# One core of attention, a gated product and an ELU layer: w_out converted first, two PSUM banks for its product, a planner that parks nothing at the shared port, and 150 priorities from a table

## The chip, the cores and the metric

The kernel runs on one core of a Trainium2 chip. Its metric is the device time of one execution in microseconds (us); the profile gives the span, from the first to the last instruction, and the time of the same execution beside it. TensorE is called PE here, VectorE DVE, ScalarE ACT, GpSimd POOL, and SyncE, which issues all DMAs of this kernel, SP.

## What is computed

Three layers in a row: block-causal attention (4 batches, 8 heads, 576 positions of 64 values), then `((x w1) * (x w2)) w3 w_out`, then an ELU layer of 2048 hidden values. All inputs are fp32.

```python
B, H, S, D = q.shape                                  # 4, 8, 576, 64
scores = scale * np.matmul(q, k.transpose(0, 1, 3, 2))
mask = block_i >= block_j                             # blocks of 64 positions
attn = softmax(np.where(mask, scores, -1000000000.0)) # in words: exp(s - max) / (sum + 1e-09)
attn_out = np.matmul(attn, v)
x = attn_out.transpose(0, 2, 1, 3).reshape(B * S, H * D)      # 2304 x 512
h = ((x @ w1) * (x @ w2)) @ w3
x = h @ w_out                                         # w1, w2: 512x1024, w3: 1024x1024, w_out: 1024x512
h = x @ w_in                                          # 512x2048
g = np.where(h > 0.0, h, np.exp(np.minimum(h, 0.0)) - 1.0)
out = g @ w_out2                                      # 2048x512
```

## The kernel before, in words

Every fp32 product runs as three faster matmuls on a rounded high part and a remainder (`PASSES`). So each operand is split: activations on the way (a cast, then a subtraction), weights by `convert`, in units of 128x512. A unit is loaded by SP as 64-bit words into one of four places (tile `cr`), ACT does one or two passes over it (L315, L322), DVE three (L328, L331, L336, with the middle result `cp` in a PSUM bank for the first units), POOL one (L345 where the exact value is kept, tile `full`; L342 where it is split further), and two more passes write the halves of a split weight (L373 on ACT, L351 on POOL or DVE).

The stages are these.

- **Attention** treats two heads at a time: 16 calls of `attention`, called pairs below, four per batch. A pair has four score groups of growing width and a last block (tile `s`, L483 and L538), row maxima on DVE (L501, L546), exponentials on ACT (L508, L558), transposes on PE (tile `t`, L518), and the product with v (tile `o`, L599). Reciprocals go through DRAM (`scr`, `rr`) to be spread over partitions, and POOL scales the result into `xy` (L650).
- **The product of w3 and w_out** is formed once, by `w_product` in eight calls of eight plain fp32 matmuls each (tile `wps`, L666), since `(...) w3 w_out` needs only `w3 w_out`. Before, all eight calls share bank 6, so each waits until ACT (L677) and DVE (L680) have read the one ahead. A call needs two converted units of w3 and all eight of w_out.
- **block2** does the gated layer in eight blocks of 288 tokens, t = 0 to 7: `xs` is the split input (L707 on DVE, L712 on POOL), `a` and `b` the two products (L767), `y` the product with `w3 w_out` (L731), which ACT or DVE (L751) adds up in `xy`. While `few` holds, `a`, `b` and `y` have one bank each; then two.
- **block3** does the ELU layer in six blocks of 384 tokens: `xa`/`xb` inputs (L813 on DVE), `h` (L839), `e` on DVE and ACT (L851, L855, L860), `o` (L874).

The order of all this isn't written out. Each helper records its operations with `add` (engine, estimated time, what it reads and writes, a priority `prio`, smaller first), numbered in the order of recording (`o.n`). `Plan.run` then walks through an estimated time line: for each engine it takes the ready operation of the smallest priority, and issues the one that can start first. Each engine runs its instructions in that order. An operation with `port=True` is taken to need the port that DVE and POOL share; in `run` it starts no earlier than the other engine's last such operation ends. Some operations may go to either of two engines (`ways`).

Where PE has nothing to do in the first part, `filler` puts in matmuls on zeros (tile `spare`, L975), one for each 0.22 us of the estimated gap. The first matmul of `w_product` sets `plan.filler = None`, and no filler follows it.

Priorities before: pairs 0 to 3 -2500, `w_product` -2400 and up, the units of w_out and w3 -1000 and up (`cp`), those of w1 and w2 behind them, pairs 4 to 15 from 40 up, block2 from 10000, block3 from 100000. The conversion of the third layer's weights waits for the end of all attention (`gate1`).

Of the kernel before, what the change touches and what calls it, by code (L numbers as in the profile page):

```python
# [37 lines left out]


COL = 13 / 12 / 2400  # L40


class Buf:
# [38 lines left out]
class Plan:  # L82
# [6 lines left out]
    def add(self, eng, us, fn, r=(), w=(), prio=0.0, port=False, after=(), lag=0.0, nbytes=0, ways=()):  # L89

        o = Op()
        o.eng, o.us, o.fn, o.prio, o.lag, o.nbytes = eng, us, fn, prio, lag, nbytes
        o.ways = {e: x for e, *x in ((eng, us, fn, port), *ways)}
        o.n = len(self.ops)
        deps = set(after)
        for key in r:
            if key in self.writer:
# [27 lines left out]
    def run(self):  # L125
# [5 lines left out]
        free = dict.fromkeys(engines, 0.0)  # L131
# [6 lines left out]
        while done < len(self.ops):  # L138
            best = None
            for e in engines:  # L140
                if not ready[e]:
                    continue
                t = max(free[e], min(o.ready for o in ready[e]))
                o = min((o for o in ready[e] if o.ready <= t), key=lambda o: (o.prio, o.n))
                if o.ways[e][2]:
                    t = max(t, port["POOL" if e == "DVE" else "DVE"])
                if best is None or t < best[0]:
                    best = t, e, o
            t, e, o = best
# [27 lines left out]
def attention_moe_moe2(  # L177
# [11 lines left out]
    nc = tc.nc  # L189
# [51 lines left out]
    def turn(name, ks, base):  # L241
        n = turns.get(name, 0)
        turns[name] = n + 1
        return bank(ks[n % len(ks)], base)
# [411 lines left out]


    def w_product(i, prio):
        ps = turn("w", (6,), "wps")
        for j in range(KF):  # L660

            def mm(j=j):
# [10 lines left out]
        def d():  # L673
            return wsl(W_S + i // 2).rearrange("p s (j c) -> p s j c", c=DM)[:, :, i % 2, :]

        k = [(slab_buf[W_S + i // 2], x, i % 2) for x in range(2)]
        add("ACT", 0.58, lambda: nc.scalar.copy(d()[:, 0, :], ps()), r=[ps], w=[k[0]], prio=prio)  # L677
        add(
            "DVE", 0.68,
            lambda: nc.vector.tensor_tensor(out=d()[:, 1, :], in0=ps(), in1=d()[:, 0, :].bitcast(F32), op=ALU.subtract),  # L680
            r=[ps, k[0]], w=[k[1]], prio=prio,
        )


# [12 lines left out]
    def block2(t):  # L697
# [17 lines left out]
                r=[(x, k, "n"), (xs, k, 0)], w=[(xs, k, 1), (x, k, "s", h2)], prio=fast, port=True,  # L715
            )
        gs = []
        few = t < 4
        abanks, bbanks, ybanks = ((5,), (6,), (7,)) if few else ((5, 0), (6, 1), (7, 3))
        nm_ = "" if few else "+"  # L720

# [195 lines left out]
    for h in range(2):  # L917
        for s in range(4):
            c = slice(h * 256, (h + 1) * 256)
            convert(  # L920
                wo_r[s][:, :, c], lambda x, s=s, c=c: full(WO_S, s).rearrange("p (j c) -> p j c", c=DM)[:, :, c],
                [[full_keys(WO_S, s)[h]]], cp, True,
            )

    def w12_units(ms, prio):
# [107 lines left out]
```

## Time and profile before

| what | value |
|---|---|
| median of 3 runs | 1012.65 us (1009.61 to 1014.29) |
| the profiled execution | 1009.9 us, span 1008.1 us |
| PE busy | 973.1 us, 97% of the span |
| DVE, ACT, POOL busy | 51%, 42%, 40% |
| mean granted PE clock | 0.993 of 2.4 GHz |

Matmuls are pipelined, and a filler counts as busy, so PE's share doesn't tell how much of the span is needed work. What PE does not need is its idle time, the fillers and what a lower granted clock costs.

### The profile page before, as it was taken

Reading aid. Unit: us, or ns where it says so; the run is one execution under the profiler, and the core shown is the slowest. Engines: PE = TensorE matmul, PEld = TensorE weight load, DVE = VectorE, ACT = ScalarE, POOL = GpSimd, SP = SyncE. Lnnn points to the kernel's source line nnn. Section 1 sums busy time; section 2 is a strip of 40 time slices with the busy share of each in tenths; the row PEclk is TensorE's granted clock in tenths of the full one; section 3 lists DMA queues with packets and bytes.
Section 4 is the critical chain, followed back from the end, with each engine's and each line's share of the span. In section 5 each row is a group of like instructions: output and inputs, shape, how many; then the busy total and the mean of one; then the engine's idle time right before and its main releaser. Section 6 shows DMA issues by size and latency. Waiting matters only on the chain.

```text
span 1008.1 us, 16417 instructions
## 1 busy us (share of the span) xinstructions
PE 973.1 (97%) x6271; PEld 837.7 (83%) x6271; DVE 514.9 (51%) x998; ACT 425.2 (42%) x1017; POOL 401.0 (40%) x403
## 2 busy tenths in 40 slices
PE   9989799999999998999999999999999999999997
PEld 4544348888888898899999988888889988999996
DVE  6888798666565646677566142232332322422222
ACT  6676576655565534544544212222222222222222
POOL 4444565333233136767677232232232422322222
PEclk9999999999999999999999999999999999999999
DMA  6554652221221112355644860000000000000000
GB/s 222 172 162 160 195 169 88 72 73 48 72 71 49 37 55 84 126 172 175 210 157 166 300 243 1 1 32 1 1 32 1 22 11 1 32 1 1 33 1 31
DMA packets 39678, 87.64 MB, mean 87 GB/s; under 512 B 3744, under 2 KB 13360, under 8 KB 38064
## 3 DMA queue, kind: packets, MB, share of 16 engines
q1 hardware_dynamic: 39600, 86.60, 25.9%
q8 instruction: 49, 0.80, 0.3%
q14 instruction: 29, 0.24, 0.1%
HBM read 69.21 MB, written 17.38 MB: 86 GB/s over the span
## 4 chain that ended last, share of the span: by engine, by line
PE 83%; DVE 9%; DMA 4%; issue 1%; ACT 1%; POOL 1%; SPq 0%; POOLq 0%; ACTq 0%; DVEq 0%
PE o L874 20%; PE h L839 20%; PE b L767 10%; PE a L767 10%; PE y L731 9%; PE o L599 4%; PE s L483 3%; PE t L518 3%; DMA cr<-w 2%; DVE ct L336 1%; PE spare L975 1%; DMA scr<-rs 1%; DVE ct L328 1%; PE wps L666 1%; PE s L538 1%
## 5 line engine op out<-in xcount | busy, mean ns | idle before, releaser
L693 POOL TENSOR_TENSOR g<-e,g 128x384 fp32r<-128x384 f32 x96 | 97.6, 1017 | 277.8 <-ACT g L690 266.0
L851 DVE TENSOR_SCALAR e<-h 128x384 f32<-128x384 f32 x96 | 53.5, 557 | 225.3 <-PE h L839 224.8
L874 PE MATMUL o<-slab_lo,g 128*128 128x512 f32 x648 | 160.5, 396 | 0.8 <-POOL g L693 0.4
L855 ACT ACTIVATE e<-e 128x384 f32<-128x384 f32 x96 | 50.4, 525 | 241.8 <-DVE e L851 241.8
L874 PEld LDWEIGHTS o<-slab_lo,g 128*128 128x128 f32 x648 | 121.2, 188 | 26.7 <-POOL g L693 0.8
L731 PE MATMUL y<-g,slab_lo 128*128 128x288 f32 x768 | 120.4, 301 | 6.6 <-DVE xy L751 6.5
L767 PE MATMUL a<-xs,slab_lo 128*128 128x288 f32 x768 | 118.2, 298 | 0.0
L767 PE MATMUL b<-xs,slab_lo 128*128 128x288 f32 x768 | 117.3, 297 | 0.8 <-DVE af L784 0.8
L731 PEld LDWEIGHTS y<-g,slab_lo 128*128 128x128 f32 x768 | 107.4, 190 | 8.5 <-DVE xy L751 7.6
L767 PEld LDWEIGHTS b<-xs,slab_lo 128*128 128x128 f32 x768 | 106.7, 188 | 1.4 <-DVE af L784 1.0
L767 PEld LDWEIGHTS a<-xs,slab_lo 128*128 128x128 f32 x768 | 107.6, 189 | 0.3 <-issue 0.2
L693 POOL TENSOR_TENSOR g<-af,g 128x288 fp32r<-128x288 f32 x64 | 55.2, 863 | 114.4 <-ACT g L690 112.7
L342 POOL TENSOR_TENSOR ct<-ct,cr 128x512 int32<-128x512 int32 x48 | 67.1, 1398 | 35.5 <-DVE ct L336 17.8
L839 PE MATMUL h<-xa,slab_lo 128*128 128x384 f32 x432 | 80.6, 336 | 0.0
L839 PE MATMUL h<-xb,slab_lo 128*128 128x384 f32 x432 | 80.1, 339 | 0.0
L860 DVE SCALAR_TENSOR_TENSOR e<-e,h 128x384 f32<-128x384 f32 x96 | 53.2, 554 | 52.3 <-ACT e L855 52.2
L839 PEld LDWEIGHTS h<-xb,slab_lo 128*128 128x128 f32 x432 | 75.9, 188 | 2.9
L839 PEld LDWEIGHTS h<-xa,slab_lo 128*128 128x128 f32 x432 | 75.8, 188 | 2.9
L690 ACT CAST g<-e 128x384 fp32r<-128x384 f32 x96 | 49.3, 513 | 62.4 <-DVE e L860 61.8
L508 ACT ACTIVATE p<-s,st 128x128 f32<-128x128 f32 (+3 forms) x128 | 66.9, 528 | 14.9 <-DVE st L501 11.2
L501 DVE TENSOR_REDUCE st<-s 128x1 f32<-128x128 f32 (+3 forms) x128 | 57.4, 481 | 25.6 <-PE s L489 25.4
L666 PE MATMUL wps<-full,full 128*128 128x512 f32 x128 | 60.6, 617 | 9.3 <-DVE slab_lo L680 5.2
(90 smaller groups left out, 1479.8 us busy)
## 6 DMA issues: line engine op xcount, KB each, us to landing
cr<-w SPq DMA_DIRECT2D x48, 512.0 KB
wsc<-stage SPq DMA_DIRECT2D x24, 512.0 KB
slab_lo<-wsc SPq DMA_DIRECT2D x12, 1024.0 KB
cr<-w3T SPq DMA_DIRECT2D x16, 512.0 KB
raw<-qT SPq DMA_DIRECT2D x16, 288.0 KB
raw<-kT SPq DMA_DIRECT2D x16, 288.0 KB
rr<-scr SPq DMA_DIRECT2D x32, 144.0 KB
out<-ob SPq DMA_DIRECT2D x17, 256.0 KB
```

The costliest lines, as they stand in the source:

```text
L342: nc.gpsimd.tensor_tensor(out=t(), in0=t(), in1=words()[0], op=ALU.add)
L501: lambda s=s, c=c: nc.vector.tensor_reduce(out=nm(c), in_=s()[:, 0:nk], axis=AX.X, op=ALU.max, negate=True),
L508: lambda s=s, c=c, p=p: nc.scalar.activation(out=p()[:, 0:nk], in_=s()[:, 0:nk], func=AF.Exp, bias=nm(c), scale=1.0, accum_out=sm(c)),
L666: nc.tensor.matmul(ps(), lhsT=a[:, j, :], rhs=bb, start=(j == 0), stop=(j == KF - 1))
L693: lambda: nc.gpsimd.tensor_tensor(out=g()[:, 1, :], in0=src(), in1=g()[:, 0, :].bitcast(F32), op=ALU.subtract),
L731: nc.tensor.matmul(ps()[:, 0:T2], lhsT=w[:, a, n * P:(n + 1) * P], rhs=gs[m]()[:, c, :], start=(m == ms[0] and q == 0), stop=(m == ms[-1] ...
L767: nc.tensor.matmul(ps()[:, 0:T2], lhsT=w[:, a, u, k, :], rhs=xs()[:, k, c, :], start=(k == 0 and q == 0), stop=(k == KD - 1 and q == 2),)
L839: nc.tensor.matmul(ph()[:, 0:T3], lhsT=w[:, a, k, :], rhs=xs()[:, k, c, :], start=(k == 0 and q == 0), stop=(k == KD - 1 and q == 2),)
L851: "DVE", dve_us(T3), lambda e=e, ph=ph: nc.vector.tensor_scalar_min(e(), ph()[:, 0:T3], 0.0),
L855: "ACT", act_us(T3, True), lambda e=e: nc.scalar.activation(out=e(), in_=e(), func=AF.Exp),
L860: lambda e=e, ph=ph: nc.vector.scalar_tensor_tensor(out=e(), in0=e(), scalar=-1.0, in1=ph()[:, 0:T3], op0=ALU.add, op1=ALU.max),
L874: nc.tensor.matmul(acc(), lhsT=g()[:, a, s * P:(s + 1) * P], rhs=w[:, c, :], start=(m == 0 and q == 0), stop=(m == KG - 1 and q == 2),)
```

## The change

The edits, of which one is a table:

- `TURNS` gives 150 of the recorded operations, by number, a priority of their own. Most of the first ones lie below -2000 or between -1000 and 260, those of block2 around 9000 to 17000, those of block3 around 100000.
- The units of w_out get -3000, and so stand ahead of pairs 0 to 3.
- `w_product` has banks 6 and 7 in turn, and the two operations that empty a bank get -9000.
- `few` ends one block earlier: block t = 3 has two banks each for `a`, `b` and `y`.
- In `run` the port is part of an operation's earliest start *before* the choice: an operation that would have to wait for the port is not chosen while another ready one of its engine can start earlier.

```diff
+TURNS = {
+    116: -2497.82, 153: -665.75, 174: -2504.65, 195: -2493.34, 215: -2487.06, 242: -2495.85, 266: -2494.31,
...
+    3646: 104161, 3720: 105078, 3722: 105076, 3771: 105406, 3790: 105578, 3792: 106919,
+}
...
         o.n = len(self.ops)
+        o.prio = TURNS.get(o.n, o.prio)
...
-                t = max(free[e], min(o.ready for o in ready[e]))
-                o = min((o for o in ready[e] if o.ready <= t), key=lambda o: (o.prio, o.n))
-                if o.ways[e][2]:
-                    t = max(t, port["POOL" if e == "DVE" else "DVE"])
+
+                held = port["POOL" if e == "DVE" else "DVE"]
+                at = lambda o: max(free[e], o.ready, held if o.ways[e][2] else 0.0)
+                t = min(map(at, ready[e]))
+                o = min((o for o in ready[e] if at(o) <= t), key=lambda o: (o.prio, o.n))
...
-        ps = turn("w", (6,), "wps")
+        ps = turn("w", (6, 7), "wps")
...
-        add("ACT", 0.58, lambda: nc.scalar.copy(d()[:, 0, :], ps()), r=[ps], w=[k[0]], prio=prio)
+        add("ACT", 0.58, lambda: nc.scalar.copy(d()[:, 0, :], ps()), r=[ps], w=[k[0]], prio=-9e3)
...
-            r=[ps, k[0]], w=[k[1]], prio=prio,
+            r=[ps, k[0]], w=[k[1]], prio=-9e3,
...
-        few = t < 4
+        few = t < 3
...
-                [[full_keys(WO_S, s)[h]]], cp, True,
+                [[full_keys(WO_S, s)[h]]], -3000.0, True,
```

The table and the planner change the order on every engine, in nearly every row. Lines of the kernel after are 27 higher in most places (L666 becomes L693, L767 L794, L707 L734, L975 L1002). Three places of the new order matter below.

**Place 1: PE, inside pair 0** (tiles `o`, `t` and `s` as above; `wps` is the product of w3 and w_out). Before, from the first `o` on:

```order
L599 MATMUL o41_292<-pt019_195,v2_104 64x256 x2
L599 MATMUL o41_292<-pt019_195,v2_104 64x128 x2
L518 MATMUL t43_300<-ident_58,p40_289 128x128 x3
L538 MATMUL s44_304<-k7_119,qb0_85 128x288 x3
L538 MATMUL s47_314<-k7_119,qb0_85 128x288 x3
L518 MATMUL t49_321<-ident_58,p42_298 128x128 x4
L518 MATMUL t51_331<-ident_58,p48_319 128x128 x4
L975 LDWEIGHTS mk_87
L975 MATMUL spare_126<-mk_87 128x512
```

After, from the same `o`:

```order
L626 MATMUL o58_417<-pt037_325,v4_112 64x256 x2
L626 MATMUL o58_417<-pt037_325,v4_112 64x128 x2
L565 MATMUL s60_427<-k15_150,qb0_85 128x288 x3
L693 MATMUL wps62_437<-full10_131,full55_407 128x512 x2
L545 MATMUL t66_448<-ident_58,p63_440 128x128 x4
L545 MATMUL t68_456<-ident_58,p64_443 128x128 x4
L565 MATMUL s69_462<-k15_150,qb0_85 128x288 x3
L693 MATMUL wps62_437<-full10_131,full55_407 128x512 x2
L693 MATMUL wps62_437<-full17_154,full55_407 128x512
```

The first `wps` stands inside pair 0 instead of inside pair 2, and with it the fillers end. Ahead of this place the new order has 102 fillers: 59 ahead of the first score, 29 between it and the first transpose, then 14. Before there were 25 ahead of the first score, 5 between it and the first transpose, and 65 later, 95 in all.

**Place 2: PE, at the first matmul of block2** (`a`, from the input `xs` and the weights `slab_lo`). Before:

```order
L666 MATMUL wps291_1428<-full22_203,full168_884 128x512 x4
L666 MATMUL wps291_1428<-full58_372,full168_884 128x512 x4
L518 MATMUL t301_1470<-ident_58,p297_1454 128x128 x3
L518 MATMUL t302_1476<-ident_58,p300_1467 128x128 x4
L538 MATMUL s304_1484<-k181_931,qb0_85 128x288 x3
L538 MATMUL s305_1490<-k181_931,qb0_85 128x288 x3
L767 MATMUL a306_1496<-xs105_583,slab_lo260_1284 128x288 x6
L666 MATMUL wps308_1507<-full22_203,full168_884 128x512 x4
```

After, from the end of pair 3 (the transpose L655 is its last):

```order
L655 MATMUL t256_1293<-ident_58,st193_1002 9x128
L693 MATMUL wps242_1222<-full17_154,full55_407 128x512 x3
L693 MATMUL wps262_1314<-full10_131,full113_645 128x512 x3
L693 MATMUL wps242_1222<-full17_154,full55_407 128x512
L693 MATMUL wps262_1314<-full10_131,full113_645 128x512
...
L693 MATMUL wps270_1357<-full10_131,full113_645 128x512 x2
L693 MATMUL wps270_1357<-full17_154,full113_645 128x512 x4
...
L794 MATMUL a279_1411<-xs123_691,slab_lo239_1211 128x288 x12
```

Before, seven of the eight calls of `w_product` and nearly all of pair 4 stand ahead of the first `a`, and one call behind it. After, all eight calls do, the last 20 matmuls of them in one piece, with two calls open at once in two banks, and of pair 4 the first score group alone.

**Place 3: DVE, at the end of block2's t = 3** (`xs` is the next block's input, `ct` a weight unit, `xy<-y` empties a bank of `y`). Before:

```order
L707 CAST xs1007_5219<-xy532_2653 128x288
L751 TENSOR_TENSOR xy293_1434<-y1003_5200,xy293_1434 128x288
L707 CAST xs1007_5219<-xy532_2653 128x288 x3
L331 TENSOR_SCALAR ct1002_5197<-ct1002_5197 128x512
L336 SCALAR_TENSOR_TENSOR ct1002_5197<-cr997_5151,ct1002_5197 128x512
L751 TENSOR_TENSOR xy293_1434<-y1008_5225,xy293_1434 128x288
L328 TENSOR_SCALAR ct1009_5230<-ct1009_5230 128x512
```

After:

```order
L734 CAST xs996_5171<-xy552_2819 128x288 x2
L811 TENSOR_TENSOR af992_5152<-b991_5145,af992_5152 128x288
L778 TENSOR_TENSOR xy330_1712<-y995_5167,xy330_1712 128x288
L734 CAST xs996_5171<-xy552_2819 128x288
L778 TENSOR_TENSOR xy330_1712<-y997_5182,xy330_1712 128x288
L734 CAST xs996_5171<-xy552_2819 128x288
L778 TENSOR_TENSOR xy330_1712<-y999_5197,xy330_1712 128x288
```

The three casts and the two passes that stood between two emptyings of `y` are spread, with at most one cast between two of them.

## Rows read from the trace of the kernel before

**Rows 1.** The page, busy time by engine.

```profile
PE 973.1 (97%) x6271; PEld 837.7 (83%) x6271; DVE 514.9 (51%) x998; ACT 425.2 (42%) x1017; POOL 401.0 (40%) x403
```

**Rows 2.** Busy time by stretch: stretch, PE, weight loads, DVE, ACT, POOL, clock, DMA.

```profile
0.00:25.00 25.00, 23.02 (x132) 12.18 (x133) 15.86 (x32) 16.45 (x39) 11.94 (x26) 1.00 0.68 223
25.00:50.00 25.00, 22.70 (x187) 14.14 (x185) 20.51 (x49) 16.40 (x44) 11.95 (x11) 1.00 0.55 174
50.00:75.00 25.00, 21.75 (x144) 12.60 (x141) 22.16 (x43) 17.61 (x45) 12.10 (x11) 1.00 0.51 157
75.00:100.00 25.00, 22.63 (x118) 12.38 (x117) 22.23 (x44) 16.05 (x38) 11.34 (x9) 0.93 0.51 160
100.00:125.00 25.00, 19.52 (x66) 9.33 (x65) 17.48 (x29) 13.48 (x29) 13.95 (x12) 0.93 0.63 204
125.00:150.00 25.00, 22.81 (x80) 11.49 (x79) 23.39 (x40) 19.08 (x41) 14.78 (x12) 1.00 0.48 159
```

**Rows 3.** PE's waits from 0 to 150 us: total, times, longest.

```profile
PE wps L666 <- DVE slab_lo L680: 5.2, 3, 2.0
PE wps L666 <- POOL ct L342: 3.0, 1, 3.0
PE t L518 <- ACT p L508: 2.1, 2, 1.8
```

**Rows 4.** Timeline of PE from 0 to 160 us: start, length, what.

```profile
1.98 8.04 PE L975 MATMUL spare<-mk 128*128 128x512 bf16 x25 [1.98 <-POOL mk L903]
9.95 0.62 PE L483 MATMUL s<-k,q 64*128 64x256 f32 x6
11.64 0.27 PE L518 MATMUL t<-ident,p 128*128 128x128 f32 x1
...
32.42 2.32 PE L975 MATMUL spare<-mk 128*128 128x512 bf16 x10
...
113.44 8.49 PE L666 MATMUL wps<-full,full 128*128 128x512 f32 x16 [2.99 <-POOL ct L342]
...
132.09 0.96 PE L483 MATMUL s<-k,q 64*128 64x512 f32 x6
...
141.46 1.09 PE L518 MATMUL t<-ident,p 128*128 128x128 f32 x7
...
143.19 0.96 PE L767 MATMUL a<-xs,slab_lo 128*128 128x288 f32 x6
145.75 7.11 PE L666 MATMUL wps<-full,full 128*128 128x512 f32 x16 [1.60 <-DVE slab_lo L680]
```

**Rows 5.** DVE's groups by line, 0 to 150 us: busy, mean ns, idle ahead.

```profile
L328 DVE TENSOR_SCALAR ct<-ct 128x512 f32<-128x512 f32 x36 | 21.4, 594 | 6.6 <-ACT ct L322 6.6
...
L707 DVE CAST xs<-xy 128x288 fp32r<-128x288 f32 x4 | 5.8, 1438 | 3.9 <-POOL xy L650 3.9
L351 DVE TENSOR_TENSOR slab_lo<-ct,slab_lo 128x512 fp32r<-128x512 f32 x5 | 5.4, 1071 | 1.2 <-ACT slab_lo L373 1.2
L680 DVE TENSOR_TENSOR slab_lo<-wps,slab_lo 128x512 fp32r<-128x512 f32 x7 | 4.8, 681 | 0.0
```

**Rows 6.** Line L328 alone, 0 to 150 us: ns, smallest/median/largest.

```profile
L328 DVE TENSOR_SCALAR ct<-ct x36: 406/419/1657, 11.1 to 149.8; 128x512 f32<-128x512 f32 x36
```

**Rows 7.** Timeline of DVE at the end of block t = 3.

```profile
424.22 0.29 DVE L707 CAST xs<-xy 128x288 fp32r<-128x288 f32 x1
...
425.33 2.14 DVE L707 CAST xs<-xy 128x288 fp32r<-128x288 f32 x3
...
429.53 0.45 DVE L751 TENSOR_TENSOR xy<-y,xy 128x288 f32<-128x288 f32 x1
```

**Rows 8.** Busy time by stretch, as in rows 2, three later stretches.

```profile
372.00:384.00 12.00, 10.64 (x78) 10.17 (x77) 7.47 (x12) 6.46 (x14) 7.30 (x9) 1.00 0.14 48
424.00:432.00 8.00, 4.34 (x25) 3.88 (x25) 7.47 (x11) 2.22 (x5) 7.32 (x7) 0.89 0.37 132
594.00:604.00 10.00, 7.76 (x37) 7.07 (x36) 5.87 (x13) 1.98 (x4) 5.77 (x8) 0.85 0.48 173
```

**Rows 9.** Timeline of PE, its last matmuls.

```profile
1000.90 1.90 PE L874 MATMUL o<-slab_lo,g 128*128 128x512 f32 x7 [0.41 <-POOL g L693]
```

18 rows, old and new, of the table TURNS are left out of this document.

## The prediction

> **What bounds the kernel now.** I read the page first, for the share of each engine: PE is busy for 973.1 of 1008.1 us [rows 1], so the end moves only if PE loses less. Its needed matmuls are the same before and after. So I looked for the time in which PE does nothing needed, stretch by stretch. In the first 150 us PE is busy for 132.4 us, the sum of six stretches, and idle for 17.6, and the granted clock falls to 0.93 in two of them [rows 2]; DVE is the fullest of the others, with 22 to 23 of 25 us in three stretches. The timeline of PE shows the fillers there: 25 take 8.04 us at the start, and later ten take 2.32 with the tail of the last, so 0.22 each; the first needed `a` of block2 starts at 143.19 [rows 4]. From there PE has work at hand. Behind it there are only small holes: 1.4 us idle between 372 and 384, 3.7 between 424 and 432, 2.2 between 594 and 604 [rows 8], 0.4 at the last matmuls [rows 9].
>
> **What is lost in the first part, before.** Up to 143.2 us: idle 17.6 - 1.6 = 16.0, since the last hole, 1.60 us, lies behind the first `a` [rows 2, 4]. Fillers: 8.04 + 70 x 0.22 = 23.4. Clock: 7% of two stretches of 25 us, 3.5 [rows 2]. Together 42.9 us, so the needed work done by then is 143.2 - 42.9 = 100.3 us. The 1.6 us comes on top: 44.5 lost in all.
>
> **What is lost there after.** Place 1 of the new order tells how it begins. 59 fillers stand ahead of the first score: 8.04 + 34 x 0.22 = 15.5 us, from 1.98 on, so the first score starts at about 17.4 us instead of 9.95. With 29 more the first transpose comes at about 24.4 instead of 11.64 [rows 4]. All 102 cost 8.04 + 77 x 0.22 = 25.0 us, 1.6 more than before; with the first 2.0 us that is 27.0. The fillers' delay is what putting w_out first costs; what it buys is that `w_product` has its inputs from pair 0 on, so that the holes of pairs 0 to 3, where PE waits for exponentials, are filled with its matmuls, and no fillers are needed there.
>
> The needed work ahead of the first `a` is about what it was (place 2): one more call of `w_product`, 7.11 us, against the part of pair 4 that isn't done yet. That part is three more score groups, of up to 0.96, the last block's scores, twenty transposes at 1.09 for seven, and one product: about 7 [rows 4]. So `a` can start at 27.0 + 100.3 = 127.3 us if PE never stands still, and each us later than that is lost. Against 44.5 lost before, the gain of the first part is 44.5 - 27.0 = 17.5 us, less the wait.
>
> **How late `a` starts** is DVE's matter. Up to that place both orders give DVE 33 to 35 units of weights, four pairs and the input of block2; after, a unit or two more and most of the reductions of pair 4 less. What can shrink is the time parked at the port. L328 takes 594 ns in the mean where its median is 419: 36 x 0.175 = 6.3 us [rows 5, 6]. L707 takes 1438 ns in the mean and 0.29 us where nothing is in its way: 4 x 1.15 = 4.6 [rows 5, 7]. L351 takes 1071 against 681 of L680, which has the same size and reads one operand from PSUM: 5 x 0.39 = 1.9 [rows 5]. Together 12.8 us. None of it saved, `a` starts at 143.2 and the gain is 17.5 - 15.9 = 1.6; all of it saved, at 130.4, and the gain is 17.5 - 3.1 = 14.4. I take two thirds, `a` at 134.7 and a gain of 10.1, since the planner now avoids the collisions that it can foresee, while the two engines drift against its estimated times, and since between 100 and 125 us DVE is busy for only 17.5 of 25 [rows 2] and so waits for something else, which a better choice at the port doesn't end.
>
> The page "SBUF — State Buffer" of the Trainium skill, section "Who interferes with whom", says that the port pair of the two engines is locked for a whole instruction and that the later one blocks fully. The trace agrees: one cast takes 0.29 us, and three of them 2.14 with POOL at work beside them [rows 7]. By that rule alone the whole 12.8 us would go and the first part would gain 14.4; I keep 10.1, since the same rule lets a DVE instruction hold up POOL, which the rows of DVE do not show.
>
> The two banks are part of this sum and not a term beside it. The wait that they end, `wps` for L680, is 5.2 us in three holes, and the waits for weights, 3.0 us, come from a product that stood late [rows 3]. All 64 matmuls now stand where their inputs are ready well ahead, and the last 20, about 17.8 us (20 x 7.11 / 8), stand over the way of pair 3's reciprocals through DRAM.
>
> **The later holes.** The hole at 424 to 432 is the end of block t = 3: with one bank, the next `y` waits until DVE has done three casts and two passes over a weight unit and then emptied the bank, at 429.53 [rows 7]. It costs 8.0 - 4.34 = 3.7 us and 11% of the clock over 8 us, 0.9 [rows 8]. After, the block has two banks, and one cast at most stands between two emptyings (place 3). I count 4 of these 4.6 us. The hole at 372 to 384, 1.4 us, lies in a block that keeps one bank; nothing is counted. The one at 594 to 604, 2.2 us and 15% of the clock, is the input of the second block of the last layer: seven casts ahead of `e`, and the new order has the same seven there, so nothing. At the end the new order has 14 groups of `o` behind the last `h`, so its last wait of 0.4 us [rows 9] should go.
>
> **The sum.** 10.1 + 4 + 0.4 = 14.5, from 1009.9 of the profiled execution: 995.4 us. That execution lies 2.75 us under the median of the runs shown, at their lower end; I say 995.
>
> **The rivals.**
> (1) DVE keeps its pace: the first `a` stays near 143, because it is loads and in-order queues that set it, and half of the later hole remains. For it speaks 100 to 125 us, where DVE is a third idle; against it, the stretches around it, where DVE is full [rows 2]. Gain 1.6 + 2 = 3.6, so about 1007.
> (2) Slower. The fillers end at about 31 us, at the start of 100 us in which PE lives on `w_product` and pairs. Where it stood still for 2.99 us before, the next product took 8.49 instead of 7.11 us, and the stretches around it had 0.93 of the clock [rows 2, 4]. Such a hole costs 2.99 + 1.38 = 4.4. With the first pair 12 us later, four holes eat up the 17.5 us, and six, 26 us, pass all terms together, 21.9: slower from the sixth hole on, and with seven, 31 us, 1019. For it: holes of 1.6 to 3.0 us in the first 150 us [rows 3, 4]. Against it: place 2 has `wps` in reserve up to the last matmul ahead of `a`. The page "TensorE: Matmul & The Clock Gate" of the same skill, section "A second HAM failure mode: psum-queue depth-cycling", says that short idle times between bursts can make the clock swing between its two levels, and that this lowers the throughput; the 8.49 us agree with it, and by it the product's bursts among transposes would be this rival. In the trace, fillers or not, the clock stayed at 1.00 from 25 to 75 us with 5.6 us idle in small holes [rows 2].
> (3) More than forecast: all parked time goes, and the holes at 372 and 594 close too (1.4, and 2.2 with 1.5 of clock). Gain 14.4 + 4.6 + 5.1 + 0.4 = 24.5, so about 985.
> (4) Nothing: PE's holes move from one place to another, and the sum stays. Then 1010 to 1013.
>
> **Chances.** The forecast 0.58; (1) 0.14, (2) 0.07, (3) 0.13, (4) 0.08. The forecast's own range is 1.6 to 14.4 and up to 4.6 of the hole, so 990 to 1003. To leave out 2 in 10, I go from 984, which keeps (3), to 1008, which keeps (1) and leaves out (2), (4). A change of this kernel can be told from none at about 0.5%, 5 us: faster means under 1007.6. The forecast and (3) are faster, (1) for the most part, in all 0.82; within 0.5% the rest of (1) and (4), 0.11; slower 0.07.
>
> **What would show it.** The first score of the kernel after at 17 us, the first transpose at 24, the first `a` between 130 and 140 us; 102 fillers; idle of PE in the first 150 us at 5 to 10 us in place of 17.6; no wait of `wps` for L707, L734 at under 0.8 us in the mean where L707 had 1.4. No wait of `y` for DVE over 2 us at t = 3, and the hole of the second block of the last layer still there, with 2 us. I am wrong if `a` starts after 143 us, if the clock is under 0.9 in several stretches between 30 and 130 us, or if a new wait of over 3 us stands behind 150 us, above all for the third layer's weights, whose units now end at the last `y` of block2 instead of a block earlier.

## The result, and the profile after

The changed kernel takes 975.40 us (median of 4 runs, 975.08 to 975.89) where the kernel before takes 1012.65: the ratio is 0.9636, 95% interval 0.9613 to 0.9659. The forecast was 995 with 984 to 1008; the change brought 37 us instead of 18, and the time lies below the range. The profiled execution took 975.89 us, span 974.1, so 34.0 us less span than before.

Page of the changed kernel, busy time by engine; then its busy time by stretch, with the columns of [rows 2]:

```profile
PE 964.2 (99%) x6278; PEld 834.3 (86%) x6278; DVE 507.6 (52%) x1008; ACT 424.2 (44%) x1014; POOL 390.1 (40%) x396
```

```profile
0.00:25.00 25.00, 23.03 (x105) 10.16 (x105) 16.75 (x28) 14.31 (x26) 16.22 (x28) 1.00 0.85 292
25.00:50.00 25.00, 25.00 (x168) 14.76 (x166) 22.00 (x46) 21.27 (x56) 8.98 (x9) 1.00 0.54 176
50.00:75.00 25.00, 22.50 (x135) 12.76 (x135) 20.01 (x42) 16.99 (x44) 10.95 (x11) 1.00 0.58 185
75.00:100.00 25.00, 25.00 (x156) 14.28 (x155) 22.32 (x49) 18.94 (x48) 15.04 (x14) 1.00 0.47 152
100.00:125.00 25.00, 25.00 (x102) 12.56 (x101) 23.25 (x40) 16.84 (x33) 17.25 (x15) 1.00 0.66 207
125.00:150.00 25.00, 24.94 (x179) 20.93 (x177) 23.78 (x40) 18.36 (x44) 12.61 (x11) 1.00 0.35 117
```

PE is idle for 4.5 of the first 150 us where it was idle for 17.6, and the granted clock stays at 1.00. Idle in the whole span: 974.1 - 964.2 = 9.9, before 1008.1 - 973.1 = 35.0. So behind 150 us it fell from 17.4 to 5.4. All of PE's waits in the changed kernel (total, times, longest), the answer to [rows 3] and to the holes of [rows 8]:

```profile
PE t L545 <- ACT p L535: 2.2, 2, 1.7
PE spare L1002 <- POOL mk L930: 2.0, 1, 2.0
PE s L510 <- ACT p L585: 0.8, 1, 0.8
PE b L794 <- DVE af L811: 0.5, 1, 0.5
PE y L758 <- DVE xy L778: 0.3, 1, 0.3
```

No wait of `wps` is left, and none of `h`. The timeline of PE up to the first `a`, the answer to [rows 4]:

```profile
1.97 15.52 PE L1002 MATMUL spare<-mk 128*128 128x512 bf16 x59 [1.97 <-POOL mk L930]
17.42 0.62 PE L510 MATMUL s<-k,q 64*128 64x256 f32 x6
...
24.29 0.27 PE L545 MATMUL t<-ident,p 128*128 128x128 f32 x1
...
110.17 17.33 PE L693 MATMUL wps<-full,full 128*128 128x512 f32 x40
127.43 0.63 PE L510 MATMUL s<-k,q 64*128 64x256 f32 x6
...
128.03 1.86 PE L794 MATMUL a<-xs,slab_lo 128*128 128x288 f32 x12
```

The first `a` starts at 128.03 instead of 143.19, 15.2 us earlier.

**Where the 34 us came from.** One number splits a span in two: the needed work that PE has done by 150 us, that is its busy time less the fillers and less what the clock cost. For the kernel after it is 145.5 - 25.3 - 0 = 120.2; before 132.4 - 25.3 - 3.5 = 103.6 (the fillers by the group of L975, 25.3 us busy, where the forecast had worked out 23.4). So the first part brought 16.6, and that is 13.1 us of idle time and 3.5 of clock. The rest of the span, span - 150 + needed work, is 944.3 after and 961.7 before: 17.4 from behind 150 us. The forecast had 10.1 and 4.4.

### The profile page after: what moved, and what is told of

It reads as the page before. It is cut to its first block, busy times and chain, and to the rows that moved or that the text cites. A ratio compares the mean times of both kernels' runs of the same rounds, so it can differ in the third digit from the quotient of the medians.

```text
span 974.1 us, 16415 instructions
## 1 busy us (share of the span) xinstructions
PE 964.2 (99%) x6278; PEld 834.3 (86%) x6278; DVE 507.6 (52%) x1008; ACT 424.2 (44%) x1014; POOL 390.1 (40%) x396
## 4 chain that ended last, share of the span: by engine, by line
PE 94%; DMA 2%; DVE 2%; issue 1%; ACT 0%; POOL 0%; SPq 0%; POOLq 0%; DVEq 0%; ACTq 0%
PE h L866 21%; PE o L901 21%; PE y L758 11%; PE a L794 10%; PE b L794 9%; PE o L626 5%; PE wps L693 5%; PE s L510 4%; PE t L545 4%; PE spare L1002 3%; PE s L565 1%; DMA wsc<-stage 1%; PE t L596 1%; DMA cr<-w3T 1%; DVE ct L363 0%
## 5 line engine op out<-in xcount | busy, mean ns | idle before, releaser
L901 PE MATMUL o<-slab_lo,g 128*128 128x512 f32 x648 | 163.0, 396 | 0.0
L794 PE MATMUL b<-xs,slab_lo 128*128 128x288 f32 x768 | 118.8, 298 | 0.6 <-DVE af L811 0.5
L794 PE MATMUL a<-xs,slab_lo 128*128 128x288 f32 x768 | 117.8, 298 | 0.0
L794 PEld LDWEIGHTS b<-xs,slab_lo 128*128 128x128 f32 x768 | 106.8, 188 | 1.6 <-DVE af L811 1.0
L794 PEld LDWEIGHTS a<-xs,slab_lo 128*128 128x128 f32 x768 | 106.6, 188 | 1.0 <-issue 0.7
L866 PE MATMUL h<-xb,slab_lo 128*128 128x384 f32 x432 | 82.1, 338 | 0.0
L369 POOL TENSOR_TENSOR ct<-ct,cr 128x512 int32<-128x512 int32 x48 | 67.9, 1420 | 34.5 <-DVE ct L363 16.8
L693 PE MATMUL wps<-full,full 128*128 128x512 f32 x128 | 59.6, 596 | 0.0
```

Of the source, the lines that this page charges most:

```text
L369: nc.gpsimd.tensor_tensor(out=t(), in0=t(), in1=words()[0], op=ALU.add)
L693: nc.tensor.matmul(ps(), lhsT=a[:, j, :], rhs=bb, start=(j == 0), stop=(j == KF - 1))
L794: nc.tensor.matmul(ps()[:, 0:T2], lhsT=w[:, a, u, k, :], rhs=xs()[:, k, c, :], start=(k == 0 and q == 0), stop=(k == KD - 1 and q == 2),)
L866: nc.tensor.matmul(ph()[:, 0:T3], lhsT=w[:, a, k, :], rhs=xs()[:, k, c, :], start=(k == 0 and q == 0), stop=(k == KD - 1 and q == 2),)
L901: nc.tensor.matmul(acc(), lhsT=g()[:, a, s * P:(s + 1) * P], rhs=w[:, c, :], start=(m == 0 and q == 0), stop=(m == KG - 1 and q == 2),)
```

## Experiments

Two theories on the first part stood after the result. **A (reserve)**: PE's holes in the first part close because the product of w3 and w_out always has matmuls at hand, whatever DVE parks. **B (the forecast's own)**: DVE's time sets the first `a`, and what the change saves there is time parked at the port. Every run was also read for the second question, which edit closes the later holes. "Needed" and "rest" are worked out as above, from each run's own profile.

| kernel | median us | span | PE busy, fillers, clock in 150 us | needed | rest |
|---|---|---|---|---|---|
| before | 1012.65 | 1008.1 | 132.4, 25.3, 3.5 | 103.6 | 961.7 |
| rule of choice alone | 1001.26 | 1001.1 | 136.1, 26.1, 6.8 | 103.2 | 954.3 |
| + second bank | 996.80 | 996.8 | 139.0, 26.1, 3.2 | 109.7 | 956.5 |
| + w_out first | 989.73 | 985.6 | 145.0, 25.3, 0 | 119.7 | 955.4 |
| + two banks at t = 3 (all but the table) | 982.52 | 981.6 | 143.8, 25.5, 1.8 | 116.6 | 948.2 |
| + table = after | 975.40 | 974.1 | 145.5, 25.3, 0 | 120.2 | 944.3 |

Each step of this ladder pays in the median: 11.4, 4.5, 7.1, 7.2 and 7.1 us, together 37.25. The runs are from several chips, on which the kernel before has medians of 1010.85 to 1012.70; by the ratios to the kernel before on the same chip (0.9913, 0.9856, 0.9793, 0.9709, 0.9636) the steps are about 9, 6, 6, 8 and 7 us. "Second bank" means two banks and the early emptying, which no run takes apart on the kernel before; no run has the table alone. How far one profile scatters is seen in two runs that keep the order of another kernel up to the middle of block2: with the banks at t = 3 alone on the kernel before, "needed" differs by 2.6 us and the first `a` comes 3.0 us earlier; with one bank each at t = 3 on the kernel after, 1.0 and 1.7 us.

**The ladder's runs**

Rule of choice alone (before, with the new lines in `run`):

```diff
-                t = max(free[e], min(o.ready for o in ready[e]))
...
+                at = lambda o: max(free[e], o.ready, held if o.ways[e][2] else 0.0)
+                t = min(map(at, ready[e]))
...
```

> The kernel before with the new rule of choice alone. Theory A (nothing to put into PE's holes, so less parking on DVE doesn't help): the first a stays after 140 us; 1005 to 1012 us. Theory B (the forecast's own step): two thirds of 12.8 us of parking go, the first a near 135, and 998 to 1004 us.

1001.26 us (ratio 0.9913, 0.9884 to 0.9942). B's time, and not for B's reason: the first `a` stays at 144.23, and needed work by 150 us is what it was. The gain is in the rest, 7.4 us. The window of the hole at 594, before and with the rule:

```profile
560.00:620.00 60.00, 57.76 (x364) 55.02 (x363) 16.53 (x35) 13.15 (x29) 16.27 (x21) 0.97 0.58 218
```

```profile
560.00:620.00 60.00, 60.00 (x376) 56.88 (x375) 16.75 (x36) 13.46 (x29) 16.52 (x21) 1.00 0.54 197
```

The rule of choice closes it alone; the hole of 372 stays (1.8 us idle between 370 and 385).

Rule of choice and second bank (no w_out first), with the edit of the banks here in part; and the same with w_out first:

```diff
-        ps = turn("w", (6,), "wps")
+        ps = turn("w", (6, 7), "wps")
...
-        add("ACT", 0.58, lambda: nc.scalar.copy(d()[:, 0, :], ps()), r=[ps], w=[k[0]], prio=prio)
+        add("ACT", 0.58, lambda: nc.scalar.copy(d()[:, 0, :], ps()), r=[ps], w=[k[0]], prio=-9e3)
...
```

> The kernel before with the rule of choice and two banks for the product, emptied early; no w_out first, no table, no second banks in block t = 3. If w_out first pays beside the rule of choice: 994 to 1000 us, since the same with w_out first gave 989.7, and needed work done by 150 us of 112 to 115 against 120. If w_out first pays only with the table: 988 to 992 us, and 117 to 120.

> The kernel before with the rule of choice, w_out first, two banks for its product and early emptying, but neither the table nor the second banks in block t = 3. If the two edits add up (11.4 and 15.9 us alone, against 1012.65): 984 to 987 us. If the second banks are worth the 4 us of the forecast beside them, 986 to 988, since all edits but the table gave 982.5; if they are worth 1 us, as in the run that took them away from the changed kernel, 982 to 984.

996.80 and 989.73 us. The first run has the time of its first case, with needed work just under it (109.7, not 112). So without the table too w_out first adds 10.0 us of needed work beside the other two edits. The second run gained less than any of its ranges said; it still has the hole at the end of t = 3 (between 385 and 440 us `y` waits for DVE three times, 4.5 us), which the next step, everything but the table, closes:

```diff
-        few = t < 4
+        few = t < 3
```

> The changed kernel without the table of 150 priorities; all other edits stay. Theory A (reserve: PE sets the pace of the first part, since the product of w3 and w_out has its inputs from pair 0 on): the start stays as it is, 102 fillers, first score near 17.4 us, all 64 product matmuls ahead of the first a, PE idle under 7 us in the first 150 us; the time lost is in later holes, so 980 to 990 us. Theory B (the vector engine's parking at the shared port set the pace, and the rule of choice ended it): the rule is still in, so 975 to 979. Theory C (the table did most of it): PE's idle time in the first 150 us is back over 12 us, 995 or more.

982.52 us, theory A's range; C falls. But half of what is lost against the kernel after, 3.6 us, lies in the first 150 us and not in later holes, as A had it. The banks at t = 3 are worth 7.2 us here, not 1 and not 4.

**Single edits on the kernel before**

W_out first with the second bank; each of them alone; w_out first with the rule of choice, without the second bank. The edit of w_out (the others as above):

```diff
-                [[full_keys(WO_S, s)[h]]], cp, True,
+                [[full_keys(WO_S, s)[h]]], -3000.0, True,
```

> The kernel before with w_out first, two banks for its product and the early emptying of these, and nothing else. Theory A: the reserve fills pairs 0 to 3 whatever DVE parks; the first a near 130 us, PE idle under 8 us in the first 150 us; 15 us less the 3 us of 20 more fillers, so 995 to 1000 us. Theory B: parking stays as it was, so the first a near 140 us and 1006 to 1012 us.

> The kernel before with w_out first and nothing else: one bank for its product, emptied at the old priority. If the early supply of weights is what ends DVE's idle time and gives the reserve: the first a near 132 us, DVE idle for under 20 us ahead of it, and 997 to 1001 us, most of the 15.9 us of both edits. If a reserve needs the second bank: wps waits for DVE over 5 us in all, the first a at 136 us or later, 1002 to 1007 us.

> The kernel before with two banks for the product, emptied early, and nothing else. If supply is what counts: only the waits of wps for L680 go, 5.2 us in all, the first a at 139 us or later, 1006 to 1011 us. If the bank is what counts: the first a near 133 us and 998 to 1002 us.

> The kernel before with the rule of choice and w_out first, one bank for its product emptied at the old priority. If the loss of w_out first alone came from the later holes of an unlucky order that the rule of choice avoids: 994 to 1001 us, not slower than the rule of choice alone (1001.3). If w_out first costs time whenever the product has one bank: 1003 to 1010 us.

Then two banks at t = 3 and nothing else:

> The kernel before with two banks each for a, b and y from block t = 3 on, and nothing else. Forecast's step: the hole at 424 to 432 goes, 4 of 4.6 us, so 1006 to 1009 us where before has 1011 to 1012. Rival: the hole is set by DVE's passes over the third layer's weights and only moves: 1010 to 1013 us.

| kernel | median us | span | PE busy, fillers, clock in 150 us | needed | rest |
|---|---|---|---|---|---|
| w_out first and second bank | 996.75 | 997.3 | 144.2, 27.6, 1.8 | 114.8 | 962.1 |
| w_out first alone | 1020.82 | 1018.5 | 137.4, 27.8, 5.2 | 104.4 | 972.9 |
| second bank alone | 1001.39 | 1001.1 | 142.2, 25.0, 1.8 | 115.5 | 966.6 |
| rule of choice and w_out first | 1007.36 | 1007.7 | 136.2, 24.2, 5.2 | 106.7 | 964.4 |
| two banks at t = 3 alone | 1008.07 | 1001.1 | 135.1, 25.4, 3.5 | 106.2 | 957.3 |

W_out first and second bank: A's range; the first `a` at 128.89, nearly as after, and no gain in the rest. Of the two, the second bank makes the first part on this kernel, 11.9 us, in the range for "the bank is what counts", and the first `a` comes at 132.44. W_out first alone gives 0.8 there and loses 11 behind, so that the kernel is slower than before (1.0071, 1.0046 to 1.0095), which no expectation had. Its window around the end of t = 3, and the same window after:

```profile
385.00:440.00 55.00, 46.85 (x304) 45.70 (x305) 36.82 (x56) 22.34 (x45) 32.55 (x29) 0.85 0.28 87
```

```profile
385.00:440.00 55.00, 55.00 (x415) 55.00 (x414) 38.19 (x65) 28.99 (x60) 33.69 (x31) 1.00 0.37 125
```

That is 8.2 us idle and 15% of 55 us of clock; the kernel before has 5.8 us and 3% there. So an edit of the first part re-plans the later orders too. Beside the rule of choice it costs 6 us against the rule alone (1007.36, ratio 0.9967, 0.9949 to 0.9985), as expected if it costs time whenever the product has one bank; that loss too lies in the rest. The two banks at t = 3 alone gave 3.1 us in the medians of one chip (1011.19 to 1008.07; ratio 0.9971, 0.9950 to 0.9992), in the forecast's range and near its 4; the profile in the table is the fastest of its ten runs, 5 us under their median, so its row shows more than that.

**Single edits taken away from the kernel after**, each alone, in the order of the diff (the first is `run`'s old rule)

> The changed kernel with the old rule of choice in the planner: the wait for the port is no longer part of an operation's earliest start. Theory A: the first part loses little, 2 to 5 us by 13 more fillers and some late product matmuls; 977 to 985. Theory B (the forecast's own step): DVE parks 12.8 us again, L355 back to 0.59 us in the mean from 0.49, and the first a comes 8 us or more later than at 128 us with PE standing still ahead of it; 984 to 992.

> The changed kernel with one bank for the product of w3 and w_out instead of two. Theory A: half of the reserve is gone, since a call waits until DVE has emptied the one bank; waits of wps for DVE of about 5 us in all come back, some holes of pairs 0 to 3 open: 979 to 986. Theory B: DVE's work and its parking are as before this edit, so 975 to 978.

> The changed kernel with the units of w_out at their old priority, behind pairs 0 to 3. Theory A: no product matmul can fill pairs 0 and 1, so fillers spread through them, PE is idle for 10 us or more in the first 150 us and the first a comes after 138 us: 985 to 993. Theory B: DVE has the same work in another order and the rule of choice keeps it from parking: 974 to 979, by up to 2 us better since the first score isn't held up by fillers.

> The changed kernel with one bank each for a, b and y in block t = 3 too, as before. Forecast's step: the hole at the end of that block comes back, 4 to 5 us, so 979 to 981 us. Rival: in the new order the casts are spread in any case and one bank is enough, so 975 to 977 us.

```diff
...
-                at = lambda o: max(free[e], o.ready, held if o.ways[e][2] else 0.0)
-                t = min(map(at, ready[e]))
...
+                t = max(free[e], min(o.ready for o in ready[e]))
...
-        ps = turn("w", (6, 7), "wps")
+        ps = turn("w", (6,), "wps")
...
-                [[full_keys(WO_S, s)[h]]], -3000.0, True,
+                [[full_keys(WO_S, s)[h]]], cp, True,
...
-        few = t < 3
+        few = t < 4
```

| kernel | median us | span | PE busy, fillers, clock in 150 us | needed | rest |
|---|---|---|---|---|---|
| old rule of choice | 989.71 | 988.2 | 137.8, 27.6, 5.0 | 105.2 | 943.4 |
| one bank for the product | 986.74 | 984.1 | 138.0, 25.0, 0 | 113.0 | 947.1 |
| w_out at its old place | 984.70 | 983.6 | 139.8, 25.4, 3.5 | 110.9 | 944.5 |
| one bank each at t = 3 | 976.63 | 974.5 | 146.2, 25.0, 0 | 121.2 | 945.8 |

All four keep the rest at 943 to 947: with the table, no single other edit is needed for the later holes, and the banks at t = 3 are worth only 1.2 us. The first three lose in the first part. One bank (the early emptying stays): `wps` waits for DVE's L707 (L680 before) again, 5.2 us in five waits, as A said; the time is just above A's range. w_out late: the first `a` at 134.88, less late than A said, the time just under its range. The old rule has B's time, again elsewhere than B said: DVE does park, even more than B had it (L354 takes 780 ns in the mean), and yet the first `a` starts at 129.35; PE stands still behind it. DVE's group up to the first `a`, the timeline of PE and the window:

```profile
L354 DVE TENSOR_SCALAR ct<-ct 128x512 f32<-128x512 f32 x35 | 27.3, 780 | 0.8 <-ACT ct L348 0.7
```

```profile
131.71 0.20 PE L515 MATMUL s<-mb,mk 64*128 64x64 bf16 x2
140.12 1.57 PE L544 MATMUL t<-ident,p 128*128 128x128 f32 x5 [8.21 <-ACT p L534]
```

```profile
125.00:150.00 25.00, 16.79 (x93) 12.87 (x92) 18.03 (x32) 12.82 (x31) 11.27 (x10) 0.80 0.43 125
```

When the product is used up, its reserve is gone, and pair 4's exponentials are late. The table was made for another rule, so this run prices the two together.

**DVE's time, made longer** (the clamp of L355 done twice in some units, the same result and the same order):

```diff
-            eng.tensor_scalar(out=a, in0=a, scalar1=HI_MIN, scalar2=HI_MAX, op0=ALU.max, op1=ALU.min)
+            for _ in range(2 if u < 24 else 1):     # or: 2 if 16 <= u < 40 else 1
+                eng.tensor_scalar(out=a, in0=a, scalar1=HI_MIN, scalar2=HI_MAX, op0=ALU.max, op1=ALU.min)
```

> The changed kernel with one DVE pass of each of the first 24 weight units (L355, 0.42 us) done twice; the second does the same again, and the order of all else is unchanged. DVE gets 24 x 0.42 = 10.1 us more work, all of it in the first 95 us. Theory A (DVE has slack there and PE sets the pace with its reserve of product matmuls): the first a within 3 us of 128.0, and 975 to 981 us. Theory B (DVE's time sets when a can start, the forecast's own step): the first a at 136 us or later, and 983 to 988 us.

> The changed kernel with the doubled DVE pass in units 16 to 39 instead of 0 to 23: the same 10.1 us more DVE work, but all of it behind the time in which the reserve of product matmuls is built up. Theory A (what hurt in the run with the first 24 units was the start, where PE has no product yet and waits for the first pairs): the reserve covers it, 976 to 980 us. Theory B (any time of DVE ahead of the first a counts, wherever it lies): 984 to 988 us.

> The kernel before with the same doubled DVE pass (L328) for its first 24 weight units, 10.1 us more DVE work. Theory B (DVE's time sets the first part of before, the premise of the forecast): the first a 8 us or more later than at 143.2, and 1018 to 1026 us. Theory A (before, PE lacks matmuls for other reasons, and DVE has slack): the first a within 4 us of 143.2, and 1010 to 1016 us.

986.70 and 990.66 us on the kernel after, 1019.78 on the one before. The first `a` moved from 128.03 to 140.03 and 139.04, and from 143.19 to 151.71; needed work by 150 us fell by 13.2, 10.9 and 8.0. B's time in all three (the second loses even more than its 984 to 988, 5.2 us of it behind 150 us), and A by itself falls: the reserve doesn't cover a slower DVE. But DVE got more than the 10.1 us that were meant. L355, with 24 passes more, in the first of these runs:

```profile
L356 DVE TENSOR_SCALAR ct<-ct 128x512 f32<-128x512 f32 x58 | 41.1, 711 | 0.9
```

That is 24.7 us more than the 16.4 of the 34 passes after: the median pass takes 0.43 us, but single ones up to 1.54. In the second run 17 passes more, ahead of the first `a`, cost 19.7 us; in the third 24 cost 25.3. A part went into DVE's idle time, which fell by 9.0, 5.9 and 10.1 us up to the first `a`. So DVE isn't full there; still `a` comes 8.5 to 12.0 us later. In the kernel after PE waits for DVE nowhere in the first 150 us; with the first 24 units doubled it does, 6.1 us in all (for `pt`, `rs` and `k`). The first part is balanced, not covered. The doubled pass is also a link in the conversion of its unit, so these runs don't tell DVE's time as a whole from the time that a unit takes.

**Fillers** (the changed kernel without them, the first line; with one for each 0.25 us of a gap, the second):

```diff
-            if e == "PE" and self.filler:
+            if e == "PE" and self.filler and False:
...
-                self.filler(int((t - free[e] - 0.3) / 0.22))
+                self.filler(int((t - free[e] - 0.3) / 0.25))
```

> The changed kernel without its 102 fillers. If the fillers only delay the start: the first score near 14.0 us, right when its inputs are there, and the clock as before, so 971 to 974 us. If the needed work of the start is then done at a lower granted clock: the first 25 or 50 us show under 0.9, and 977 to 983 us.

> The changed kernel with a filler for each 0.25 us of an estimated gap instead of 0.22: 90 fillers instead of 102, 52 ahead of the first score. The first score 1.5 us earlier, at about 15.9 us, the first transpose about 2.4 us earlier at most, the clock still 1.00; 973 to 975 us if that passes through to the end, the same 975 if DVE's time sets the first a.

976.20 and 975.12 us (972.79 to 975.64): neither differs from 975.40 by more than 1 us, and the first lies between its two ranges (what its second case asks of the clock can't be read from the column, as the last section shows). 25 us of fillers bring at most 0.8 (by the ratios, 0.9632 and 0.9636, nothing). Without them the first `a` comes at 129.37; with 90 at 126.09, 2 us earlier, in the profiled run, which is the fastest of its five. That is no more than the scatter: the run with one bank each at t = 3 has the same 102 fillers and order there, and 126.29. No version tried beats the changed kernel beyond that scatter.

## Why the forecast missed

**What held.** The first score at 17.42 (forecast 17.4), the first transpose at 24.29 (24.4), 102 fillers, the waits of `wps` gone, the last wait gone, no wait of `y` over 2 us. Needed work ahead of the first `a`: 127.2 busy - 25.3 - 3.5 = 98.4 before, 123.6 - 25.3 = 98.3 after, so the same, as place 2 was read. The earliest `a`, 127.3, which came 0.7 us later, is right by luck: the fillers before cost 25.3 us and not 23.4, so the needed work was put at 100.3, 1.9 too high. With 98.4 the same sum gives 125.7 (98.4 + 25.3 + 2.0), and four of the kernels tried have `a` between 125.3 and 126.9.

**The step that failed first: "What can shrink is the time parked at the port."** The premise, that DVE's time sets the first `a`, is borne out by the three runs with more DVE work. But two things shrank, not one, and the first `a` doesn't follow the one that was priced. Stretch up to the first `a`, before, after, and in the kernel without the table; DVE is the third busy time:

```profile
0.00:143.19 143.19, 127.21 (x701) 69.39 (x702) 114.96 (x218) 94.24 (x222) 74.44 (x78) 0.98 0.57 182
```

```profile
0.00:128.03 128.03, 123.56 (x670) 65.78 (x670) 107.29 (x206) 90.68 (x207) 69.89 (x75) 1.00 0.62 204
```

```profile
0.00:126.91 126.91, 123.48 (x670) 66.05 (x671) 112.08 (x199) 89.67 (x206) 67.27 (x71) 1.00 0.61 196
```

DVE's groups there, after:

```profile
L355 DVE TENSOR_SCALAR ct<-ct 128x512 f32<-128x512 f32 x34 | 16.4, 484 | 2.6 <-ACT ct L349 2.4
L378 DVE TENSOR_TENSOR slab_lo<-ct,slab_lo 128x512 fp32r<-128x512 f32 x6 | 4.8, 798 | 0.5 <-ACT slab_lo L400 0.4
L734 DVE CAST xs<-xy 128x288 fp32r<-128x288 f32 x4 | 4.0, 988 | 2.5 <-POOL xy L677 2.5
```

By the forecast's own prices parked time is 34 x 0.065 + 6 x 0.117 + 4 x 0.70 = 5.7 us after, where it was 12.8 before: 7.1 saved, near the 8.5 (two thirds) of the forecast. Of the other 8.1 of the 15.2 us, 7.5 are idle time of DVE, 143.19 - 114.96 = 28.2 before and 128.03 - 107.29 = 20.7 after, and 0.6 is the rest of its busy time. The forecast had seen the idle time ("DVE is busy for only 17.5 of 25") and held it for fixed.

Saved parking is neither needed nor enough for an early `a`. The same two terms, worked out in the same way up to the first `a` of each kernel:

| kernel | first `a` | parked | DVE idle | both |
|---|---|---|---|---|
| before | 143.19 | 12.8 | 28.2 | 41.0 |
| rule of choice alone | 144.23 | 8.9 | 30.0 | 38.9 |
| second bank alone | 132.44 | 8.3 | 26.2 | 34.5 |
| w_out first alone | 137.95 | 12.2 | 19.4 | 31.6 |
| all but the table | 126.91 | 12.3 | 14.8 | 27.1 |
| after | 128.03 | 5.7 | 20.7 | 26.4 |
| after, with the old rule | 129.35 | 15.4 | 12.5 | 27.9 |

Without the table DVE parks as long as before, and with the old rule longer, and `a` comes 14 to 16 us earlier all the same. The rule of choice alone saves 3.9 us of parking, and `a` doesn't move. So the rule does not by itself keep DVE from parking on the chip, and DVE that parks less waits more. What goes down with `a`, to about 4 us, is the sum of both; what is left of the time, 98 to 106 us, is DVE's work and what its other lines are parked.

What ends the idle time is w_out first. In each of the five pairs of kernels that differ in this edit alone it falls: from 28.2 to 19.4 on the kernel before, from 26.2 to 16.9 beside the second bank, from 30.0 to 26.1 beside the rule of choice, from 26.7 to 15.3 beside both, and from 25.7 to 20.7 from w_out at its old place to the kernel after. The first `a` comes 3.6 to 9.8 us earlier in these pairs. That is not yet time gained: on the kernel before the needed work by 150 us grows by 0.8 alone. How, the start of DVE shows, before and after:

```profile
5.08 1.38 DVE L450 SCALAR_TENSOR_TENSOR k<-raw,k 128x576 fp32r<-128x576 f32 x1 [5.08 <-ACT k L438]
8.55 0.43 DVE L324 TENSOR_SCALAR ct<-cr 128x512 int32<-128x512 int32 x1 [2.09 <-DMA cr<-wo]
11.05 0.42 DVE L328 TENSOR_SCALAR ct<-ct 128x512 f32<-128x512 f32 x1
```

```profile
4.61 0.43 DVE L351 TENSOR_SCALAR ct<-cr 128x512 int32<-128x512 int32 x1 [4.61 <-DMA cr<-wo]
5.08 0.43 DVE L355 TENSOR_SCALAR ct<-ct 128x512 f32<-128x512 f32 x1
12.25 1.75 DVE L477 SCALAR_TENSOR_TENSOR k<-raw,k 128x576 fp32r<-128x576 f32 x1
```

Before, DVE waits for the first `k`, then for w_out's load, and does its first L328 at 11.05. After, it waits for the load of w_out alone, starts on a unit at 4.61 and has done four when it takes the first `k` at 12.25. Its later waits for ACT's first pass fall too, from 6.6 us in four to 2.4 in one:

```profile
DVE ct L328 <- ACT ct L322: 6.6, 4, 3.2
```

```profile
DVE ct L355 <- ACT ct L349: 2.4, 1, 2.4
```

Why these fall stays open. The second bank was put at nothing of its own ("part of this sum and not a term beside it"), and alone it brings `a` 10.8 us earlier: `wps` no longer waits for L680, and ahead of `a` PE does all eight calls of the product and of pair 4 the first score group alone, so that DVE has 203 instructions there instead of 218. Together the terms that were left out made the first part 16.6 instead of 10.1.

The page "SBUF — State Buffer" of the Trainium skill, section "Who interferes with whom", has the lock of the port; by that rule alone, as the forecast worked it out, all 12.8 us would have gone, and 5.7 stayed in the kernel after. That one cast takes longer beside POOL, as the page has it, is still in the rows above: 988 ns in the mean for L734, where the same cast took 0.29 us with nothing in its way [rows 7].

**The step that cost most: "Behind it there are only small holes."** The four holes named make 7.7 us; the page and the windows that the forecast cites leave 35.0 - 17.6 = 17.4 us idle behind 150 us. The sum was never closed. Of the 9.7 us left over, 5.7 lie at the end, from 990 on, and 2.1 between 384 and 424. And of the holes named, two that were set at nothing went. For 594 the forecast said "the new order has the same seven there, so nothing". The casts are the same; what stands on PE ahead of the waiting `h` is not. PE at that place, before and after:

```profile
594.86 3.28 PE L839 MATMUL h<-xa,slab_hi 128*128 128x384 f32 x18
600.38 1.85 PE L839 MATMUL h<-xa,slab_hi 128*128 128x384 f32 x6 [2.24 <-DVE e L860]
```

```profile
567.67 4.37 PE L866 MATMUL h<-xa,slab_hi 128*128 128x384 f32 x24
571.88 1.57 PE L901 MATMUL o<-slab_hi,g 128*128 128x512 f32 x6
573.28 2.34 PE L866 MATMUL h<-xa,slab_hi 128*128 128x384 f32 x12
```

After, six `o` lie between, 1.4 us, and the bank of `h` is free in time. With the rule of choice alone nine `o` stand there, and the hole is closed too. The hole of the one-bank block at 372 is gone as well: between 330 and 385 PE is busy for all 55 us. Together the later part brought 17.4 instead of 4.4: 12.0 us of idle time, 7.1 - 3.5 = 3.6 of clock (mean 0.993 of 1008.1 us, of which 3.5 lie in the first part; after, 1.000), and 1.8 that no row names. By the ladder it is the rule of choice (7.4), the banks at t = 3 (7.2) and the table (3.9), less 1.1 that the second bank and w_out first lose. A difference of 3 us between two profiles can be scatter. With the table in, any one of the others can be taken away and the rest stays at 943 to 947; without the table it is 948.2.

**The rivals.** Rival 3 (more than forecast) had the direction and the places, but with 7.7 us of holes instead of 17.4 it ended at 985. Rival 2's holes after the fillers did not come: the granted clock is 1.00 in every stretch up to 150 us. The page "TensorE: Matmul & The Clock Gate" of the Trainium skill, section "A second HAM failure mode: psum-queue depth-cycling", describes such a swing; no row after shows one. Of the signs named, four were wrong: the first `a` between 130 and 140 (128.03), PE idle for 5 to 10 us of the first 150 (4.5), L734 under 0.8 us (0.99 over its first four), and the hole of the last layer's second block still there (gone).

## What to carry to other kernels

Before pricing single holes, close the sum: span less busy time, by stretch, must equal the holes named, and what is left over gets a line of its own in the forecast. When one engine sets the pace, count its idle time beside its slow instructions; idle time ends when work is put where it waits, here it was as large a term as the parking, and parking saved can come back as waiting. Whether a hole closes is read from the waiting engine's own order (what now stands ahead of the wait), not only from the engine waited for. Price a new edit beside the others, since w_out first loses 8 us alone and gains 7 beside two others.

## What the runs showed of the hardware

Without fillers the first matmuls take 1.6 to 1.7 times as long, and the column of the granted clock doesn't show it. A window of the kernel without fillers, its timeline (six scores of 64x512, three transposes), and the same matmuls after:

```profile
30.00:34.00 4.00, 3.77 (x16) 2.28 (x18) 2.63 (x5) 2.79 (x8) 2.93 (x3) 1.00 0.67 227
```

```profile
31.06 1.65 PE L510 MATMUL s<-k,q 64*128 64x512 f32 x6
32.72 0.90 PE L545 MATMUL t<-ident,p 128*128 128x128 f32 x3
```

```profile
30.05 0.96 PE L510 MATMUL s<-k,q 64*128 64x512 f32 x6
30.99 0.55 PE L545 MATMUL t<-ident,p 128*128 128x128 f32 x3
```

Two product matmuls (four in the rows) right behind them take 1.88 us in both, at 35.37 and at 32.77. PE had been idle for most of the time before 23 us in the first kernel and busy with fillers in the second. The column reads 1.00 (2.4 GHz) in the window above, but it takes off only what the trace records as lower, and the records of the clock begin at 34.6 us in this trace, at 7.3 in the one after. So of this start the column says nothing; that the clock stood at its lower level, 1.2 GHz, up to there fits the lengths and is not recorded. The cost can be read: up to the first `a` PE is busy for 104.4 us with 568 recorded matmuls, where after it spends 123.6 - 25.3 = 98.3 on the same 568. So the fillers bring 6.1 us, and cost 4.8: with them PE spends 25.3 + 4.5 = 29.8 us on fillers and idle time up to `a`, without them 25.0 on idle time. That is why taking them away moves `a` by 1.3 us only.
